# Sparse attention and a feed-forward layer: another PSUM bank for one first product, and two gates kept in SBUF

## The chip, the cores and the metric

The kernel runs on one core of a Trainium2 chip. The metric is the device time of one execution in microseconds (us). The engines go by their names in the profile: PE is TensorE (matmul), PEld its weight load, DVE is VectorE, ACT is ScalarE, POOL is GpSimd, SP is SyncE, from which this kernel issues its DMAs.

## The reference, cut to what matters

Two kinds of sparse attention (heads 0 to 3: a local window of 32 keys; heads 4 to 7: every 32nd key), and behind it a feed-forward layer with a piecewise quadratic gate. The change touches the gate and its neighbours alone.

```python
def _moe_ref(x, w_in, w_out):          # x: 4608 x 512, from the attention
    h = x @ w_in                       # w_in: 512 x 2048
    neg, pos = h <= -1.0, h >= 1.0
    g = np.where(pos, h, np.where(neg, 0.0, (h + 1.0) ** 2 / 4.0))
    return g @ w_out                   # w_out: 2048 x 512
```

## The kernel before

The feed-forward layer works through the 4608 tokens in nine chunks `c` of 512 (`CH`), and in each chunk through the 2048 hidden columns in sixteen blocks `f` of 128 (`NF`). A pair (c, f) is called a unit here; "unit 2" is (0, 2), the third of the first chunk.

A unit has three steps. `up` (line 530) forms the **first product** h in one PSUM bank of 128 x 512: four slices of the contraction, each in three parts (high x high, high x low, low x high, since every float32 is split in two parts of the type fp32r), so 12 matmuls, all of line 540. `gate` (line 543) turns h into the gate: ACT forms u = relu(0.5 h + 0.5) (L549) and squares it (L550), DVE forms g = min(max(h, 1), u) (L554), a copy gives the high part gh (L558 on DVE in chunk 0, L556 on ACT later), and DVE subtracts to get the low part gl (L559). `down` (line 562) forms the **second product**: for each of four groups `t` of 128 tokens, three matmuls into a bank of its own (L570); the four banks gather over all 16 units of a chunk.

PSUM has eight banks, in three pools: four under the name "o", two under "h", two under "a". A pool gives its banks out in turn, and the first write into a bank waits until the last reader of its tenant before is done. Before the change, all first products use the two "h" banks in turn. So unit 2's first product takes the bank of unit 0's, and waits until unit 0's gate has read it. In chunk 0 the four "o" banks serve the attention of the first sequence before the second products begin; their last tenants there are the transposes of `f3` and the values of `v2`.

Where g is written decides who reads the bank last. In unit 0, g is written over u, in SBUF, so L554 is the last reader of h. In every other unit, g is written back over h, in PSUM, and L558 (or L556) and L559 read it there too. The buffer u exists once (`bufs=1`), so ACT's L549 of a unit waits for the last reader of u in the unit before.

Everything is issued in an order written out by hand. In chunk 0, `begin` issues the attention of the first sequence, with the first products of units 0 and 1 mixed in. Then, for each f from 2, PE gets the first product of unit f, the attention steps of `STEPS` (in unit 2: `s0`, the scores of the second sequence), and the second product of the unit two before it (unit 0's, once three gates are pending). DVE gets, for the gate of unit 2, ahead of L554 the steps `m0` and `x0`, which are the mask addition that takes these scores out of PSUM (L353, two instructions) and the maximum (L364). Between the gates ACT, DVE and POOL also turn the weights from the input's 64-bit form into two fp32r parts: L178 and L181 (ACT), L186 (DVE), L191 (POOL), L197 (ACT, or DVE), L201 (DVE), one chain for each half of a block. Each engine takes its instructions strictly in this order, so a matmul that waits holds everything behind it on PE.

Of the kernel before, what the change touches and what calls it, by code (L numbers as in the profile page):

```python
# [17 lines left out]
P = 128  # L18
# [5 lines left out]
def tile_sparse_attention_then_ffn(  # L24
# [29 lines left out]
    B, _, _, _, S = qk_l.shape  # L54
# [5 lines left out]
    CH = 512  # L60
# [46 lines left out]
    def psum(kind, shape, name):  # L107
        pool, bufs = ps[kind]
        return pool.tile(shape, F32, tag=kind, bufs=bufs, name=name)
# [418 lines left out]
    o_ps = {}  # L528

    def up(c, f, first=True, last=True):  # L530
        r0 = c * CH % RING
        if first:
            o_ps[c, f] = psum("h", [P, CH], f"h_{c}_{f}")
        todo = [(cc, x, y) for cc in range(NC) for x, y in HI_LO]
        if not (first and last):

            todo = [(cc, 0, y) for cc in ((0, 1) if first else (2, 3)) for y in range(2)]
            todo += [] if first else [(cc, 1, 0) for cc in range(NC)]
        for n, (cc, x, y) in enumerate(todo):
            nc.tensor.matmul(o_ps[c, f], wt[f][:, x, 0, cc * P:(cc + 1) * P], xT[y][:, cc, r0:r0 + CH],  # L540
                             start=first and n == 0, stop=last and n == len(todo) - 1)

    def gate(c, f, between=lambda: None):

        hp = o_ps.pop((c, f))
        gh = g_p.tile([P, CH], F32R, tag="gh", name=f"gh_{c}_{f}")
        gl = g_p.tile([P, CH], F32R, tag="gl", name=f"gl_{c}_{f}")
        u = g_p.tile([P, CH], F32, tag="u", bufs=1, name=f"u_{c}_{f}")
        nc.scalar.activation(u, hp, AF.Relu, bias=half, scale=0.5)  # L549
        nc.scalar.activation(u, u, AF.Square)  # L550
        between()

        g = u if (c, f) == (0, 0) else hp
        nc.vector.scalar_tensor_tensor(out=g, in0=hp, scalar=1.0, in1=u, op0=ALU.max, op1=ALU.min)  # L554
        if c:
            nc.scalar.copy(gh, g)  # L556
        else:
            nc.vector.tensor_copy(gh, g)  # L558
        nc.vector.tensor_tensor(out=gl, in0=g, in1=gh.bitcast(F32), op=ALU.subtract)  # L559
        return gh, gl  # L560
# [30 lines left out]
    def begin(names):  # L591


        conv = {"A": lambda f, i: conv_a(f, i, (False,)), "L": lambda f, i: conv_a(f, i, (True,)),
                "B": conv_b, "C": conv_c, "D": conv_d, "E": conv_e,
                "G": lambda f, i: conv_d(f, i, nc.vector.tensor_copy)}
        for name in names.split():
            if name[0] in "UV":
                up(0, int(name[0] == "V"), name[1] == "0", name[1] == "1")
            elif name[0] in conv:  # L600
                conv[name[0]](int(name[1]), int(name[2]))
            else:
                first(name)

    with tc.manual_schedule():
# [36 lines left out]
        for c in range(NCH):  # L642
            b = need[c + 1] if c + 1 < NCH and need[c + 1] > need[c] else None
            go = attention(b, lambda u, kind, n: "a") if b is not None else None
            for f in range(NF):
                if c or f > 1:
                    up(c, f)
                pe, pre, mid, post = (LATER if c else STEPS).get(f, ("",) * 4) if b is not None else ("",) * 4
                if pe:
                    go(pe)  # L650
                if c == 0:
                    start_w(*halves[f])
                if pre:
                    go(pre)
                pend.append((c, f, gate(c, f, lambda: mid and go(mid))))
                if c == 0:
                    end_w(*halves[f])
                    if f == 9:
                        for i in range(2):
                            load_piece(NF - 2, i)  # L660
                        for i, k in ((0, 0), (0, 1), (1, 0)):
                            load_piece(NF - 1, i, k, o_p, "ob", 2)
                    if f == NF - 4:
                        load_piece(NF - 1, 1, 1, of=2)
                    if f == NF - 3:
                        fetch_qk(2, 0)
                if post:
                    go(post)
                n = 2 if 0 < c and (c, f) < (NCH - 1, NF - 1) else 1
                if len(pend) > 2:  # L670
                    down(*pend[:n])
                    del pend[:n]
# [61 lines left out]
```

## Time and profile before

| | us |
|---|---|
| time, median of 3 runs (lowest, highest) | 881.38 (881.37, 883.25) |
| the profiled execution, its own time | 883.73 |
| its span in the profile | 881.9 |
| PE busy | 872.9 |
| ACT busy | 398.0 |
| DVE busy | 384.6 |
| POOL busy | 114.7 |

The span is what the profiler saw between the first and the last instruction; the execution's own time includes 1.8 us around it. A row of the timeline gives the start and the duration in us, the engine, the line of the kernel, the operation, output and input by their names, the shapes, and how many instructions the row holds (x4); square brackets give the idle time ahead of it and what ended that. Matmuls overlap each other in the pipeline, so a row of four that takes 1.07 us holds four starts 0.23 us apart and the duration of the last. A row of the windows gives the stretch, its length, the busy time and the count of PE, PEld, DVE, ACT and POOL, then the granted clock of PE (1.00 is full), the busy share of the DMA engines and GB/s. A row of the groups gives the count, and the shortest, median and longest duration in ns.

### The profile page before, as it was taken

What the parts mean: (1) busy time and instruction counts of PE and PEld (TensorE: products, weight loads), DVE (VectorE), ACT (ScalarE), POOL (GpSimd) and SP (SyncE); (2) the same over time, 40 slices, a digit from 0 to 9 for tenths busy, and PEclk for the clock granted to TensorE, in tenths of its full rate; (3) what the DMA queues carried; (4) which work ended last, traced back from release to release, by engine and by line L of the source; (5) the groups of instructions that cost most, each with busy time, mean ns of one, the idle gap of its engine ahead of it and who ended that gap; (6) DMA issues with size and microseconds to landing.
All of it is one profiled execution on the core that took longest, in us unless ns stands there. A gap on an engine that the chain in (4) does not pass through costs nothing.

```text
span 881.9 us, 17353 instructions
## 1 busy us (share of the span) xinstructions
PE 872.9 (99%) x7253; PEld 710.3 (81%) x7253; DVE 384.6 (44%) x709; ACT 398.0 (45%) x732; POOL 114.7 (13%) x136
## 2 busy tenths in 40 slices
PE   8999999999999999999999999999999999999998
PEld 6788888888888888887888888888888888888886
DVE  5899854443453434434344345333453322222221
ACT  5889953434434443334434343444333433343333
POOL 6354411100120002100110011100210000000000
PEclk8999999999999999999999999999999999999999
DMA  9917331422232322421241223321222000000001
GB/s 354 405 65 242 114 121 61 140 59 60 105 100 81 83 70 72 125 64 62 81 145 52 67 105 94 87 82 49 76 82 60 33 29 1 0 35 14 1 0 48
DMA packets 41646, 77.61 MB, mean 88 GB/s; under 512 B 8800, under 2 KB 22112, under 8 KB 41568
## 3 DMA queue, kind: packets, MB, share of 16 engines
q1 hardware_dynamic: 41568, 76.50, 26.8%
q8 instruction: 57, 0.93, 0.4%
q14 instruction: 21, 0.17, 0.1%
HBM read 59.18 MB, written 17.30 MB: 87 GB/s over the span
## 4 chain that ended last, share of the span: by engine, by line
PE 95%; DMA 1%; ACT 1%; DVE 1%; SPq 1%; issue 0%; ACTq 0%; DVEq 0%
PE o L570 44%; PE h L540 44%; PE xp L459 3%; PE sc L302 3%; DMA qk<-in_qk_s 1%; PE tp L405 1%; SPq L443 0%; DMA pT<-there 0%; ACT u L549 0%; ACT u L550 0%; DMA there<-t 0%; DVE xTl L504 0%; DVE h L554 0%; SPq L237 0%; ACT gh L556 0%
## 5 line engine op out<-in xcount | busy, mean ns | idle before, releaser
L540 PE MATMUL h<-xTh,w 128*128 128x512 f32 x1152 | 373.2, 391 | 0.4 <-DVE u L554 0.4
L570 PE MATMUL o<-w,gh 128*128 128x512 f32 x1152 | 359.5, 393 | 0.1
L554 DVE SCALAR_TENSOR_TENSOR h<-h,u 128x512 f32<-128x512 f32 x143 | 100.0, 699 | 377.1 <-ACT u L550 377.0
L540 PEld LDWEIGHTS h<-xTh,w 128*128 128x128 f32 x1152 | 216.3, 188 | 46.6 <-DVE u L554 0.8
L570 PEld LDWEIGHTS o<-w,gh 128*128 128x128 f32 x1152 | 213.4, 188 | 45.3 <-ACT gh L556 0.6
L540 PE MATMUL h<-xTl,w 128*128 128x512 f32 x576 | 224.5, 390 | 0.4 <-DVE xTl L504 0.4
L570 PE MATMUL o<-w,gl 128*128 128x512 f32 x576 | 224.9, 390 | 0.0
L549 ACT ACTIVATE u<-h,half 128x512 f32<-128x512 f32 x144 | 99.1, 688 | 269.6 <-PE h L540 268.6
L559 DVE TENSOR_TENSOR gl<-h,gh 128x512 fp32r<-128x512 f32 x143 | 98.9, 692 | 84.6 <-ACT gh L556 83.7
L570 PEld LDWEIGHTS o<-w,gl 128*128 128x128 f32 x576 | 108.1, 188 | 25.7 <-DVE gl L559 0.6
L540 PEld LDWEIGHTS h<-xTl,w 128*128 128x128 f32 x576 | 108.1, 188 | 22.9 <-DVE xTl L504 1.1
L556 ACT CAST gh<-h 128x512 fp32r<-128x512 f32 x128 | 75.2, 587 | 100.1 <-DVE h L554 100.1
L550 ACT ACTIVATE u<-u 128x512 f32<-128x512 f32 x144 | 91.0, 632 | 4.6
L368 POOL TENSOR_TENSOR pr<-pr,st 128x768 f32<-128x768 f32 (+3 forms) x31 | 36.3, 1172 | 322.8 <-DVE st L364 307.6
L392 POOL TENSOR_TENSOR pr<-pr,st 128x648 f32<-128x648 f32 (+3 forms) x30 | 35.2, 1173 | 119.3 <-DVE st L391 118.4
L191 POOL TENSOR_TENSOR raw<-raw 128x512 uint32<-128x512 uint32 (+1 forms) x34 | 35.0, 1047 | 37.9 <-DVE raw L186 23.4
L504 DVE TENSOR_TENSOR xTl<-xp,xTh 128x216 fp32r<-128x216 f32 (+8 forms) x94 | 35.7, 442 | 6.0 <-ACT xTh L500 6.0
L383 ACT ACTIVATE st<-st 128x12 f32<-128x12 f32 (+2 forms) x32 | 6.8, 211 | 67.5 <-DVE st L379 67.4
L459 PEld LDWEIGHTS xp<-pT,v 64*64 64x64 f32 (+2 forms) x1760 | 29.0, 138 | 10.1 <-issue 8.2
L302 PEld LDWEIGHTS sc<-qk 64*32 64x32 f32 (+1 forms) x1856 | 25.9, 117 | 12.1 <-issue 10.1
L459 PE MATMUL xp<-pT,v 64*64 64x32 f32 (+2 forms) x1760 | 32.3, 224 | 1.5 <-DMA pT<-there 0.8
L500 ACT CAST xTh<-xp 128x216 fp32r<-128x216 f32 (+8 forms) x94 | 31.1, 459 | 6.0 <-DVE xTl L504 3.5
(56 smaller groups left out, 348.3 us busy)
## 6 DMA issues: line engine op xcount, KB each, us to landing
raw<-in_w SPq DMA_DIRECT2D x30, 512.0 KB, 9.6
qk<-in_qk_s SPq DMA_DIRECT2D x16, 604.0 KB, 4.9
qk<-in_qk_l SPq DMA_DIRECT2D x16, 576.0 KB, 4.8
out<-ob SPq DMA_DIRECT2D x35, 256.0 KB, 2.0
v<-in_v_l SPq DMA_DIRECT2D x21, 384.0 KB, 4.0
there<-t SPq DMA_DIRECT2D x96, 48.0 KB, 1.7
pT<-there SPq DMA_DIRECT2D x12, 384.0 KB, 3.0
v<-in_v_s SPq DMA_DIRECT2D x7, 384.0 KB, 4.4
```

The source lines that it names most:

```text
L302: nc.tensor.matmul(sc[j][i * Q:(i + 1) * Q, s, p], qk[:, 0, q0:q0 + Q], qk[:, 1, k0:k0 + W], start=u not in covered, stop=u not in covered)
L368: eng.tensor_tensor(out=pr, in0=pr, in1=st[:, 0].unsqueeze(2).broadcast_to(list(pr.shape)), op=ALU.add)
L392: eng.tensor_tensor(out=pr, in0=pr, in1=st[:, 2].unsqueeze(2).broadcast_to(list(pr.shape)), op=ALU.mult)
L459: nc.tensor.matmul(xp[p][j * D:(j + 1) * D, n], loaded[b, local, b0 + n][keys, j], qs, start=True, stop=True)
L504: nc.vector.tensor_tensor(out=dst[1], in0=src, in1=dst[0].bitcast(F32), op=ALU.subtract)
L540: nc.tensor.matmul(o_ps[c, f], wt[f][:, x, 0, cc * P:(cc + 1) * P], xT[y][:, cc, r0:r0 + CH], start=first and n == 0, stop=last and n == l ...
L549: nc.scalar.activation(u, hp, AF.Relu, bias=half, scale=0.5)
L550: nc.scalar.activation(u, u, AF.Square)
L554: nc.vector.scalar_tensor_tensor(out=g, in0=hp, scalar=1.0, in1=u, op0=ALU.max, op1=ALU.min)
L556: nc.scalar.copy(gh, g)
L559: nc.vector.tensor_tensor(out=gl, in0=g, in1=gh.bitcast(F32), op=ALU.subtract)
L570: nc.tensor.matmul(o_ps[c][t], gs[x][:, t * P:(t + 1) * P], wt[f][:, y, 1, :], start=f == 0 and n == 0, stop=f == NF - 1 and n == 2)
```

## The change

Two lines. Unit 2's first product is taken from the pool "o", so that it no longer takes the "h" bank of unit 0's; and the gates of units 1 and 2 are written over u in SBUF, as unit 0's is, rather than over h in PSUM.

```diff
     def up(c, f, first=True, last=True):
         r0 = c * CH % RING
         if first:
-            o_ps[c, f] = psum("h", [P, CH], f"h_{c}_{f}")
+            o_ps[c, f] = psum("o" if (c, f) == (0, 2) else "h", [P, CH], f"h_{c}_{f}")
...
-        g = u if (c, f) == (0, 0) else hp
+        g = u if (c, f) < (0, 3) else hp
         nc.vector.scalar_tensor_tensor(out=g, in0=hp, scalar=1.0, in1=u, op0=ALU.max, op1=ALU.min)
         if c:
             nc.scalar.copy(gh, g)
         else:
             nc.vector.tensor_copy(gh, g)
         nc.vector.tensor_tensor(out=gl, in0=g, in1=gh.bitcast(F32), op=ALU.subtract)
```

No instruction is added, removed or put elsewhere on any engine; what changes is who waits for whom. In the rows below, h_1, h_2 and h_3 are the first products of units 1, 2 and 3, w the weights, and a name in square brackets is the engine whose semaphore the instruction waits for (DVE_49 is VectorE's).

On PE, at the start of unit 2's first product, behind the last matmuls of unit 1's (- before, + after):

```order
 L540 MATMUL h_1_617<-xTh,w_585 128x512 [waits DVE_49]
 L540 MATMUL h_1_617<-xTh,w_585 128x512 x3
+L540 MATMUL h_2_697<-xTh,w_643 128x512 [waits PE_49,Activation_49]
+L540 MATMUL h_2_697<-xTl,w_643 128x512
 L540 MATMUL h_2_697<-xTh,w_643 128x512 [waits DVE_49]
-L540 MATMUL h_2_697<-xTl,w_643 128x512
-L540 MATMUL h_2_697<-xTh,w_643 128x512 x2
+L540 MATMUL h_2_697<-xTh,w_643 128x512
```

Before, its first matmul waits for DVE (the gate of unit 0, L554). After, the first matmul waits for PE and ACT alone (the bank's tenants in the attention, and the weights' high part), and the third for DVE (the weights' low part, L201).

On PE, in unit 0's second product and the start of unit 3's first (o_0 to o_3 are the four banks of the second products):

```order
-L570 MATMUL o_1_788<-w_524,gh_0_654 128x512 x2
+L570 MATMUL o_1_788<-w_524,gh_0_654 128x512 [waits PE_49]
+L570 MATMUL o_1_788<-w_524,gh_0_654 128x512
 L570 MATMUL o_1_788<-w_524,gl_0_655 128x512
 L570 MATMUL o_2_789<-w_524,gh_0_654 128x512 [waits PE_49]
 L570 MATMUL o_2_789<-w_524,gh_0_654 128x512
 L570 MATMUL o_2_789<-w_524,gl_0_655 128x512
-L570 MATMUL o_3_790<-w_524,gh_0_654 128x512 [waits PE_49]
+L570 MATMUL o_3_790<-w_524,gh_0_654 128x512 [waits DVE_49]
 L570 MATMUL o_3_790<-w_524,gh_0_654 128x512
 L570 MATMUL o_3_790<-w_524,gl_0_655 128x512
```

With unit 2's first product in front of them in the pool, the four second products move on by one bank, and the fourth comes round to the bank of unit 2's first product. Its first matmul now waits for DVE, for the instruction that reads that bank last: L554 of unit 2. Before, it waited for PE's own earlier work in the bank.

On DVE, from the gate of unit 1 to that of unit 2, after the change (gh and gl are the two parts of the gate, raw the weights as they come, pr the scores in SBUF, sc the scores in PSUM, st the maxima):

```order
L554 SCALAR_TENSOR_TENSOR u_1_686<-h_1_617,u_1_686 128x512 [waits DVE_49,Activation_49]
L558 CAST gh_1_684<-u_1_686 128x512 [waits DVE_49]
L559 TENSOR_TENSOR gl_1_685<-u_1_686,gh_1_684 128x512 [waits DVE_49]
L201 TENSOR_TENSOR w_692<-raw_183,w_692 128x512 [waits Activation_49]
L201 TENSOR_TENSOR w_585<-raw_172,w_585 128x512 [waits Activation_49]
L186 TENSOR_SCALAR raw_190<-raw_190 128x512 [waits DMAHW2_49,Activation_49]
L186 TENSOR_SCALAR raw_178<-raw_178 128x512 [waits DMAHW5_49,Activation_49]
L353 TENSOR_TENSOR pr_0_773<-sc_0_0_710,m_loc 128x384 [waits PE_49]
L353 TENSOR_TENSOR pr_0_773<-sc_0_1_711,m_loc 128x384 [waits PE_49]
L364 TENSOR_REDUCE st_0_774<-pr_0_773 128x12 [waits DVE_49]
L554 SCALAR_TENSOR_TENSOR u_2_770<-h_2_697,u_2_770 128x512 [waits Activation_49]
```

The order of these eleven rows is that of before. In the first three and the last, u stands where h stood.

## The prediction

> **What bounds the kernel now.** I read the page first: engines, then the chain that ended last.
>
> ```profile
> PE 872.9 (99%) x7253; PEld 710.3 (81%) x7253; DVE 384.6 (44%) x709; ACT 398.0 (45%) x732; POOL 114.7 (13%) x136
> PE 95%; DMA 1%; ACT 1%; DVE 1%; SPq 1%; issue 0%; ACTq 0%; DVEq 0%
> ```
>
> PE is the bound: 95% of the chain. So the question is in which places PE stands still, and whether a place comes or goes. The windows and the waits of PE answer that for everything behind the change:
>
> ```profile
> 42.00:870.00 828.00, 827.23 (x6538) 675.50 (x6537) 354.22 (x649) 365.18 (x664) 94.08 (x96) 1.00 0.24 73
> ```
>
> ```profile
> PE xp L459 <- DMA pT<-there: 0.8, 1, 0.8
> ```
>
> From 42 us to 870 us PE is busy for 827.23 of 828 us at full clock, and has one wait, of 0.8 us. What PE loses before 42 us is therefore not made good later (at most 0.8 us of it), and what it gains there is kept. The place itself, in order of time on PE:
>
> ```profile
> 31.02 1.07 PE L540 MATMUL h<-xTh,w 128*128 128x512 f32 x4
> 32.44 0.50 PE L540 MATMUL h<-xTh,w 128*128 128x512 f32 x1 [0.35 <-DVE u L554]
> 32.78 0.39 PE L540 MATMUL h<-xTl,w 128*128 128x512 f32 x1
> 33.01 0.62 PE L540 MATMUL h<-xTh,w 128*128 128x512 f32 x2
> ...
> 35.39 1.17 PE L302 MATMUL sc<-qk 64*32 64x64 f32 x96
> 36.49 0.72 PE L570 MATMUL o<-w,gh 128*128 128x512 f32 x2
> ...
> 38.44 0.40 PE L570 MATMUL o<-w,gl 128*128 128x512 f32 x1
> 38.67 0.62 PE L570 MATMUL o<-w,gh 128*128 128x512 f32 x2
> 39.13 0.39 PE L570 MATMUL o<-w,gl 128*128 128x512 f32 x1
> ```
>
> Unit 1's first product ends with the four matmuls from 31.02; unit 2's begins at 32.44, held until the gate of unit 0 (L554) has left its bank. Then come 96 scores (35.39) and unit 0's second product, four banks of three matmuls each; the fourth bank's three begin at 38.67. Next, VectorE over the same stretch:
>
> ```profile
> 31.70 0.69 DVE L554 SCALAR_TENSOR_TENSOR u<-h,u 128x512 f32<-128x512 f32 x1 [1.37 <-ACT u L550]
> ...
> 35.74 0.70 DVE L554 SCALAR_TENSOR_TENSOR h<-h,u 128x512 f32<-128x512 f32 x1 [0.89 <-ACT u L550]
> 36.47 0.69 DVE L558 CAST gh<-h 128x512 fp32r<-128x512 f32 x1
> 37.20 0.69 DVE L559 TENSOR_TENSOR gl<-h,gh 128x512 fp32r<-128x512 f32 x1
> 37.81 1.28 DVE L201 TENSOR_TENSOR w<-raw,w 128x512 fp32r<-128x512 f32 x2
> 39.01 0.76 DVE L186 TENSOR_SCALAR raw<-raw 128x512 uint32<-128x512 uint32 x2
> 39.68 1.01 DVE L353 TENSOR_TENSOR pr<-sc,m_loc 128x384 f32<-128x384 f32 x2
> 40.72 0.95 DVE L364 TENSOR_REDUCE st<-pr 128x12 f32<-128x768 f32 x1
> 41.59 0.69 DVE L554 SCALAR_TENSOR_TENSOR h<-h,u 128x512 f32<-128x512 f32 x1
> ```
>
> The three L554 rows are the gates of units 0, 1 and 2. From 35.74 to 42.28 VectorE has no gap; its only idle times are ahead of the first two gates, which wait for ScalarE. Unit 2's gate is late because nine other instructions stand between it and unit 1's.
>
> **Term 1, the wait that goes.** Four matmuls from 31.02 at the usual spacing of 0.23 us (32.78 to 33.01) end their slots at 31.93. Unit 2's first product, no longer behind unit 0's gate, could start there and not at 32.44: 0.51 us. The first matmul after the wait is followed 0.34 us later rather than 0.23, another 0.11. So 0.6 us of PE time comes free, and scores and unit 0's second product move up by as much: the fourth bank would be due at 38.67 - 0.62 = 38.05, and the third bank's last matmul would end near 38.2.
>
> **Term 2, the wait that comes.** The pool of the second products has four banks, given out in turn. Unit 2's first product takes one, the second products then take the other three and, as fourth, the very bank of unit 2's first product. The rows of the changed program say so: the fourth bank's first matmul now waits for VectorE. The last to read that bank is L554 of unit 2, which in the trace begins at 41.59 and ends at 42.28. From the end of a gate to the matmul it frees took 0.05 us (31.70 + 0.69 = 32.39, then 32.44). So the fourth bank starts near 42.33. Against 38.67 that is 3.66 us late, and with 0.11 us for the first matmul after a wait **3.8 us**. Term 1 is inside this: it makes PE arrive earlier at a wait whose end VectorE sets, and so is worth nothing. PE stands from 38.2 to 42.3, 4.1 us.
>
> Can VectorE come sooner? The gates in SBUF speed up one instruction, the cast:
>
> ```profile
> L558 DVE CAST gh<-h x4: 690/691/692, 36.5 to 54.5; 128x512 fp32r<-128x512 f32 x4
> L558 DVE CAST gh<-u x1: 426/426/426, 32.4 to 32.4; 128x512 fp32r<-128x512 f32 x1
> ```
>
> That is 0.26 us for unit 1 ahead of unit 2's gate (unit 2's own cast comes behind it). But GpSimd runs when unit 1's cast starts, and another VectorE instruction that met it was held:
>
> ```profile
> 34.64 2.10 POOL L191 TENSOR_TENSOR raw<-raw 128x512 uint32<-128x512 uint32 x2 [3.14 <-DVE raw L186]
> ```
>
> ```profile
> 51.62 1.48 POOL L392 TENSOR_TENSOR pr<-pr,st 128x768 f32<-128x768 f32 x1 [2.69 <-DVE st L391]
> ```
>
> ```profile
> L186 DVE TENSOR_SCALAR raw<-raw x1: 1705/1705/1705, 51.7 to 51.7; 128x512 uint32<-128x512 uint32 x1
> ```
>
> The L186 at 51.7 took 1.705 us, to 0.3 us behind the end of L392 at 53.10; the pair at 39.01 took 0.76 in all. L191 runs to 36.74; a cast held from 36.47 to there and then 0.43 long ends at 37.17, against 37.16 before. So the gain is between 0 and 0.26, and I take 0, since the cast's start lies inside L191. Term 2 is 3.5 to 3.8. L554 and L559 cost the same from either memory (0.69, 0.70 in the rows above). The buffer u is now read until L559, which a later gate's ScalarE pass must await; unit 1's L559 ends at 37.89, and unit 2's pass at L549 stands behind ScalarE's own work until 39.59 (L550 follows and ends at 40.95, before 41.59). No cost while ScalarE is that late; if it were free at once, the wait would end at 37.89 and still be hidden.
>
> Behind the waiting matmul stand the rest of the fourth bank, unit 3's first product, 48 scores and every later product; who waits for them:
>
> ```profile
> 41.85 0.39 PE L540 MATMUL h<-xTh,w 128*128 128x512 f32 x1
> 42.17 0.77 PE L302 MATMUL sc<-qk 64*32 64x64 f32 x48
> ```
>
> ```profile
> 45.27 0.68 ACT L549 ACTIVATE u<-h,half 128x512 f32<-128x512 f32 x1
> ```
>
> Unit 3's last matmul moves from 41.85 to about 45.6 and ends near 46.0, so ScalarE's pass of unit 3 moves from 45.27 by 0.7; the mask addition for the scores, VectorE's, by a few tenths. Both slip far less than PE does, so they are earlier relative to PE than before, and no further wait follows from them. No DMA changes place.
>
> **Term 3, the clock.** PE stands still for longer than anywhere in the trace. What a thin stretch did before:
>
> ```profile
> 6.31:9.73 3.42, 2.50 (x146) 2.03 (x146) 2.44 (x4) 0.90 (x5) 1.22 (x4) 1.00 1.02 394
> ...
> 13.14:16.56 3.42, 2.02 (x37) 1.40 (x39) 3.39 (x7) 3.36 (x10) 1.26 (x2) 1.00 1.02 393
> 16.56:19.97 3.41, 3.11 (x89) 2.64 (x82) 1.89 (x7) 2.82 (x8) 1.35 (x2) 0.50 1.03 417
> 19.97:23.39 3.42, 3.42 (x57) 3.36 (x58) 3.03 (x9) 1.28 (x4) 2.14 (x2) 0.50 1.03 409
> 23.39:26.80 3.41, 3.41 (x99) 2.80 (x98) 2.21 (x7) 2.64 (x8) 1.15 (x1) 1.00 1.03 415
> ```
>
> The granted clock halves at 16.56, behind a stretch with PE busy for 2.02 of 3.42 us, and is back at 23.39, 6.83 us later, twice 3.41; a stretch with 2.50 busy had left it alone. A standstill of 4.1 us leaves at least one stretch of 3.41 us with 1.4 us of work or less, wherever its borders fall. I therefore take the clock to halve. The price of half clock, from transposes at either rate:
>
> ```profile
> 21.46 2.34 PE L405 MATMUL tp<-ident,pr 128*128 128x128 f32 x11
> ...
> 53.91 0.82 PE L405 MATMUL tp<-ident,pr 128*128 128x128 f32 x6
> ```
>
> One takes 0.213 us in the first row (clock 0.50 but for its end) and 0.137 in the second (clock 1.00), so 36% of the work is lost at least, and half where matmuls follow each other closely, as here. One stretch of 3.41 us at half clock costs 1.2 to 1.7 us of PE time. The bounds are 0 (no drop) and 2.7 (low from 42.3 for 5.5 us, when the stretch that holds the restart is too thin to bring the clock back). I take 1.6, one full stretch near half.
>
> **Sum.** 3.8 + 1.6 = 5.4 us. Against the profiled execution's 883.73 us (span 881.9) that is 889.1; that execution lies 2.4 us above the median of the runs shown, so against 881.38 us the forecast is **886.8 us**.
>
> **Rivals.**
> *The clock stays up*: 3.8 us alone, 885.2 us (884.9 with the cast's full gain). For it speaks the end of the span:
>
> ```profile
> 876.73:880.14 3.41, 1.48 (x7) 0.89 (x5) 0.00 (x0) 1.86 (x5) 0.00 (x0) 1.00 0.75 274
> 880.14:881.90 1.76, 0.00 (x0) 0.00 (x0) 0.00 (x0) 0.00 (x0) 0.00 (x0) 1.00 0.21 65
> ```
>
> A stretch with 1.48 us of work was not followed by a lower clock in the record. Against it: 2.02 us of work was followed by one at 16.56, though of smaller matmuls. [...]
>
> *The new wait finds its gate done*: then only term 1 is left, 0.6 us faster, 880.8 us. Its place is the fourth bank, due at 38.05; it decides if unit 2's gate ends by 38.0. That needs VectorE 4.3 us earlier than the trace, with nine instructions of 5.1 us between it and the gate before (36.44 to 41.59); it could only be if waits, not work, filled that time, and their rows show no gap.
>
> *VectorE meets GpSimd more often*:
>
> ```profile
> 39.56 2.10 POOL L191 TENSOR_TENSOR raw<-raw 128x512 uint32<-128x512 uint32 x2 [2.82 <-ACT raw L178]
> ```
>
> The second of the L186 pair, if some tenths of a microsecond move either engine, could fall behind the first of these L191 and be held by its 1.05 us. Then the standstill ends near 43.4: 4.8 + 1.6, 887.8 us.
>
> **How the numbers follow.** The forecast has 0.52, the clock that stays up 0.36, the longer VectorE chain 0.06, the gate found done 0.04, anything else 0.02. The range runs from 884.5 (3.5 us, no drop, less some tenths between runs) to 887.9 (3.8 + 2.7). A change of 0.3%, 2.6 us, is about what a measurement of this kernel can tell from none. All cases but the gate found done lie above 884.0: slower 0.90; same 0.06 (a standstill shorter by over 1 us); faster 0.04.
>
> **What would show it.** In the new profile PE waits once, about 4 us, at L570 for DVE u L554 with its end near 42.3; the wait of L540 at 32.4 is gone; unit 2's first product starts near 31.9; the granted clock shows 0.5 for 3 to 5 us behind it. Without the dip, term 3 is wrong. If the wait ends before 41 us, the VectorE order was read wrongly; if PE idles less than before between 42 and 870 us, the loss is paid back.

## The result, and the profile after

The changed kernel takes 887.29 us (median of 4 runs, 886.25 to 889.18), the kernel before 882.32 us beside it (4 runs, 881.37 to 883.44). The ratio is 1.0065, with a 95% interval of 1.0052 to 1.0078: slower by 4.6 to 6.9 us. The forecast was 886.8 us, in a range of 884.5 to 887.9. The profiled execution took 887.41 us, with a span of 885.6.

The page of the changed kernel, engines and the costliest group of second products (busy time, mean ns, then the idle time ahead of it and what ended most of that):

```profile
PE 872.0 (98%) x7253; PEld 709.4 (80%) x7253; DVE 383.7 (43%) x709; ACT 397.7 (45%) x732; POOL 114.5 (13%) x136
...
L570 PE MATMUL o<-w,gh 128*128 128x512 f32 x1152 | 360.1, 394 | 4.1 <-DVE u L554 4.0
```

PE is as busy as before (872.0 against 872.9 us) in a span 3.7 us longer, and the second products, which had 0.1 us of idle time ahead of them, now have 4.1. The waits of PE say that this is one wait:

```profile
PE o L570 <- DVE u L554: 4.0, 1, 4.0
```

PE in order of time in the changed kernel, from the end of unit 1's first product to the scores behind unit 3's:

```profile
30.36 0.61 PE L540 MATMUL h<-xTh,w 128*128 128x512 f32 x2
30.82 0.39 PE L540 MATMUL h<-xTl,w 128*128 128x512 f32 x1
...
32.72 1.17 PE L302 MATMUL sc<-qk 64*32 64x64 f32 x96
33.82 0.72 PE L570 MATMUL o<-w,gh 128*128 128x512 f32 x2
...
35.77 0.40 PE L570 MATMUL o<-w,gl 128*128 128x512 f32 x1
40.17 1.22 PE L570 MATMUL o<-w,gh 128*128 128x512 f32 x2 [4.00 <-DVE u L554]
41.19 0.63 PE L570 MATMUL o<-w,gl 128*128 128x512 f32 x1
41.62 0.63 PE L540 MATMUL h<-xTh,w 128*128 128x512 f32 x1
42.04 0.63 PE L540 MATMUL h<-xTl,w 128*128 128x512 f32 x1
...
46.27 0.77 PE L302 MATMUL sc<-qk 64*32 64x64 f32 x48
```

No gap stands ahead of unit 2's first product any more. Three banks of unit 0's second product pass, and the fourth begins at 40.17 after 4.00 us. Behind it the matmuls start 0.42 us apart (41.62 to 42.04) where 0.23 is usual, so PE runs at about half its rate. VectorE over the same time:

```profile
33.70 0.69 DVE L554 SCALAR_TENSOR_TENSOR u<-h,u 128x512 f32<-128x512 f32 x1 [0.88 <-ACT u L550]
34.43 0.57 DVE L558 CAST gh<-u 128x512 fp32r<-128x512 f32 x1
...
38.57 0.95 DVE L364 TENSOR_REDUCE st<-pr 128x12 f32<-128x768 f32 x1
39.44 0.68 DVE L554 SCALAR_TENSOR_TENSOR u<-h,u 128x512 f32<-128x512 f32 x1
40.15 1.27 DVE L558 CAST gh<-u 128x512 fp32r<-128x512 f32 x1
```

Unit 2's gate ends at 40.12, 0.05 us before the fourth bank starts. From unit 1's gate to unit 2's are 5.74 us, 5.85 before. The granted clock (the number before the last two) in stretches of the changed kernel:

```profile
37.00:38.00 1.00, 0.00 (x0) 0.00 (x0) 1.00 (x4) 1.00 (x3) 0.60 (x1) 1.00 0.98 385
38.00:39.00 1.00, 0.00 (x0) 0.00 (x0) 0.96 (x3) 0.97 (x3) 1.00 (x2) 0.83 1.05 422
39.00:40.00 1.00, 0.00 (x0) 0.00 (x0) 1.00 (x2) 0.92 (x2) 0.83 (x2) 0.50 1.04 406
...
42.00:45.00 3.00, 3.00 (x8) 2.31 (x7) 2.89 (x6) 1.20 (x2) 1.17 (x2) 0.50 0.78 311
45.00:46.00 1.00, 1.00 (x5) 0.73 (x3) 0.00 (x0) 0.00 (x0) 0.92 (x1) 0.75 0.09 37
```

It halves at 38.66, in the middle of the wait (0.83 in that stretch: 0.66 us at 1.00, 0.34 at 0.50), and is back at 45.5. That is 6.8 us, two times the 3.41 us that a fall lasts in e8 (below). PE works at half clock in the last 5.3 us of it, from 40.17 to 45.5.

One thing makes the two spans hard to compare. In the profiled execution of the kernel before, the clock was also down from 16.56 to 23.39; in that of the changed kernel it was not (1.00 up to 38 us), so everything near 32 us comes about 2 us earlier in it. To leave this out I measure within each profile, from the scores of unit 2's step to those of four steps later (L302, 48 of 64x54). Before, these stand at 35.39 (shown in the prediction) and here:

```profile
60.12 0.92 PE L302 MATMUL sc<-qk 64*64 64x54 f32 x48
```

In the changed kernel the first set stands at 32.72 (above) and the second here:

```profile
64.20 0.92 PE L302 MATMUL sc<-qk 64*64 64x54 f32 x48
```

That is 24.73 us before and 31.48 after, 6.75 more. Unit 2's scores come 0.6 us sooner than they did (0.98 us ahead of unit 1's gate, 0.35 before), so the change costs 6.1 us over this stretch. Behind it, the two kernels run in step: the lag of the changed one stays at 4.07 to 4.09 us of the trace's time from 60 to 396 us, and at 3.83 to 3.84 from 412 us on. (It is less than 6.1 because the profile of the kernel before had lost some 2 us to its early low clock.)

### The profile page after: what moved, and what is told of

Same layout as the page of the kernel before. It is cut to its first block, busy times and chain, and to the rows that moved or that the text cites. A ratio compares the mean times of both kernels' runs of the same rounds, so it can differ in the third digit from the quotient of the medians.

```text
span 885.6 us, 17353 instructions
## 1 busy us (share of the span) xinstructions
PE 872.0 (98%) x7253; PEld 709.4 (80%) x7253; DVE 383.7 (43%) x709; ACT 397.7 (45%) x732; POOL 114.5 (13%) x136
## 4 chain that ended last, share of the span: by engine, by line
PE 94%; DMA 2%; DVE 1%; ACT 1%; SPq 1%; issue 0%; ACTq 0%; DVEq 0%
PE o L570 44%; PE h L540 44%; PE xp L459 3%; PE sc L302 3%; DMA qk<-in_qk_s 1%; PE tp L405 0%; SPq L443 0%; DMA pT<-there 0%; DMA v<-in_v_s 0%; ACT u L549 0%; ACT u L550 0%; DVE pr L353 0%; ACT raw L181 0%; DVE st L364 0%; DMA there<-t 0%
## 5 line engine op out<-in xcount | busy, mean ns | idle before, releaser
L554 DVE SCALAR_TENSOR_TENSOR h<-h,u 128x512 f32<-128x512 f32 x141 | 98.6, 699 | 379.3 <-ACT u L550 379.2
L559 DVE TENSOR_TENSOR gl<-h,gh 128x512 fp32r<-128x512 f32 x141 | 97.6, 692 | 84.9 <-ACT gh L556 83.7
L459 PEld LDWEIGHTS xp<-pT,v 64*64 64x64 f32 (+2 forms) x1760 | 28.2, 134 | 10.4 <-issue 8.6
L302 PEld LDWEIGHTS sc<-qk 64*32 64x32 f32 (+1 forms) x1856 | 25.7, 116 | 12.3 <-issue 9.4
L459 PE MATMUL xp<-pT,v 64*64 64x32 f32 (+2 forms) x1760 | 31.6, 221 | 1.8 <-ACT pT L415 0.7
```

The costliest lines, as they stand in the source:

```text
L302: nc.tensor.matmul(sc[j][i * Q:(i + 1) * Q, s, p], qk[:, 0, q0:q0 + Q], qk[:, 1, k0:k0 + W], start=u not in covered, stop=u not in covered)
L459: nc.tensor.matmul(xp[p][j * D:(j + 1) * D, n], loaded[b, local, b0 + n][keys, j], qs, start=True, stop=True)
```

## The experiments

The last column of this table is the same measure for every profile: the time between the two sets of scores, less 24.73, and less the 0.62 of term 1 where unit 2's first product uses the other bank (there the first set comes that much sooner, which lengthens the time between the sets and is no loss).

| kernel | median us (runs) | ratio to before, 95% interval | between the scores, us | cost there, us |
|---|---|---|---|---|
| before | 881.5 to 882.3 in three sets | | 24.73 | |
| changed | 887.29 (4) | 1.0052 to 1.0078 | 31.48 | +6.1 |
| e1, bank alone | 889.8 (6) | 1.0064 to 1.0105 | 32.42 | +7.1 |
| e2, gates alone | 881.76 (12) | 0.9986 to 1.0009 | 24.77 | 0.0 |
| e3, wait filled | 886.48 (8) | 1.0028 to 1.0058 | 29.08 | +3.7 |
| e4, gate first | 886.68 (6) | 1.0046 to 1.0083 | 29.29 | +3.9 |
| e5, bank later | 882.63 (12) | 0.9990 to 1.0015 | 25.24 | -0.1 |
| e6, before, early places filled | 882.16 (11) | 0.9994 to 1.0012 | 24.77 | 0.0 |
| e8, changed, early places filled | 887.39 (5) | 1.0052 to 1.0077 | 30.64 | +5.3 |
| e9, both fillings | 886.71 (5) | 1.0042 to 1.0069 | 29.05 | +3.7 |

The theory: the loss is PE's wait at the fourth bank for unit 2's gate, and a halved clock behind that wait. The first rival: the gates in SBUF cost it. The second: the wait is all, and the clock is a symptom.

### e1: the bank alone

```diff
-        g = u if (c, f) < (0, 3) else hp
+        g = u if (c, f) == (0, 0) else hp
```

> The bank alone: unit 2's first product in the fourth bank of the second products, the gates of units 1 and 2 written over h in PSUM as before. Theory (the loss is PE's wait for the last reader of that bank, and a halved clock behind it): the last reader is now L559 of unit 2, two instructions of 0.69 us behind L554, so PE stands about 1.4 us longer than the 4.0 us of the changed kernel, and the time is 888.7 us (887.8 to 889.8) against 887.3. Rival (the loss comes from gates in SBUF that meet GpSimd): without those gates the time falls back to 882.3 to 884.

889.8 us, at the upper end of the range expected, and in the waits of e1 on PE:

```profile
PE o L570 <- DVE gl L559: 5.6, 1, 5.6
```

With g in PSUM, the bank is free only after L559 and the wait is 1.6 us longer, in the place that the theory names. The gates in SBUF do not cause the loss; they shorten it (6.1 us over the stretch with them, 7.1 without).

### e2: the gates alone

```diff
-            o_ps[c, f] = psum("o" if (c, f) == (0, 2) else "h", [P, CH], f"h_{c}_{f}")
+            o_ps[c, f] = psum("h", [P, CH], f"h_{c}_{f}")
```

> The gates of units 1 and 2 in SBUF alone, unit 2's first product in the bank of unit 0's as before. Theory (the bank is what costs): no wait at the fourth bank, the 0.35 us wait for unit 0's gate stays, and the time is that of before, 882.3 us (881.4 to 883.2). Rival (gates in SBUF cost): 884 us or more.

881.76 us, no difference from before, no wait at the fourth bank, and the old one of 0.3 us for unit 0's gate:

```profile
PE h L540 <- DVE u L554: 0.3, 1, 0.3
```

Together with e1 this puts the whole loss on the bank.

### e3: the wait filled with matmuls

```diff
-        if first:
+        if first and (c, f) not in o_ps:
...
+            if (c, f0, t) == (0, 0, 3):
+                o_ps[0, 3] = psum("h", [P, CH], "h_0_3")
+                for _ in range(32):
+                    nc.tensor.matmul(o_ps[0, 3][:, :256], zeros, zeros[:, :1].broadcast_to([P, 256]), start=True, stop=True)
```

> The changed kernel with 32 matmuls of zeros, 128 x 256, set ahead of the fourth bank's first matmul, into the bank that unit 3's first product takes next: PE waits for the same gate, but is busy meanwhile. Theory (two prices, the wait of 3.5 us and the halved clock of 2.5 us): the fourth bank starts as late as before, the granted clock stays at 1.00, and the time is 884.8 us (883.8 to 885.8). Rival (the wait alone is the loss, and the clock costs nothing beside it): 887.3 us as the changed kernel (886.5 or more).

PE in e3, around the fourth bank:

```profile
38.18 3.73 PE L571 MATMUL h<-zeros 128*128 128x256 bf16 x32
42.32 0.74 PE L574 MATMUL o<-w,gh 128*128 128x512 f32 x2 [0.41 <-DVE u L554]
42.90 0.40 PE L574 MATMUL o<-w,gl 128*128 128x512 f32 x1
43.14 0.40 PE L540 MATMUL h<-xTh,w 128*128 128x512 f32 x1
43.37 0.40 PE L540 MATMUL h<-xTl,w 128*128 128x512 f32 x1
```

The bank still waits for the gate, but the matmuls behind it start 0.23 us apart: the clock stays up, at 1.00 from 36 to 50 us. The cost over the stretch falls from 6.1 to 3.7 us, as the theory said. So the wait itself is worth 3.7 us and the clock, in the changed kernel's profile, 2.4. The median, 886.48, lies above the 883.8 to 885.8 that I expected and 0.02 us short of the rival's 886.5, so it does not decide between them. The expectation left out the early fall of the clock. The eight runs fall in two groups: four with a mean clock of 0.999 or 1.000 take 884.4 to 885.8 us, four with 0.996 take 887.1 to 887.7 (see e6); the profile shown is of the second group.

### e4: the gate of unit 2 first

```diff
-        STEPS = {2: ("s0", "", "m0 x0", "a0"), 3: ("s1", "e0 q0", "p0 m1 x1", "a1 r0"), 4: ("", "e1 q1", "p1", "r1"),
+        STEPS = {2: ("s0", "", "", "m0 x0 a0"), 3: ("s1", "e0 q0", "p0 m1 x1", "a1 r0"), 4: ("", "e1 q1", "p1", "r1"),
...
+                if (c, f) == (0, 2):
+                    pend.append((c, f, gate(c, f)))
                 if c == 0:
                     start_w(*halves[f])
...
-                pend.append((c, f, gate(c, f, lambda: mid and go(mid))))
+                if (c, f) != (0, 2):
+                    pend.append((c, f, gate(c, f, lambda: mid and go(mid))))
```

> The changed kernel with the gate of unit 2 issued ahead of the weight conversions of that step on ScalarE, VectorE and GpSimd, and the mask addition and maximum (L353, L364) behind the gate. Theory (the place of unit 2's gate in VectorE's order sets how long PE stands): ScalarE's passes of unit 2 come some 2.2 us sooner, L554 of unit 2 ends about 2.7 us sooner, PE stands 1.2 to 1.6 us instead of 4.0, the clock stays at 1.00 behind it, and the time is 883.5 us (882.3 to 884.8), if the conversions put off by 2 us are not late for PE. Rival (the standstill has another end than that gate): 4.0 us as before and 887.3.

The wait is shorter, as it should be if the place of the gate sets it; the waits and the clock of e4:

```profile
PE o L570 <- DVE u L554: 1.8, 1, 1.8
```

```profile
39.00:40.00 1.00, 1.00 (x5) 0.80 (x4) 1.00 (x3) 0.78 (x2) 0.07 (x1) 0.76 1.04 414
40.00:42.00 2.00, 2.00 (x6) 1.52 (x5) 0.36 (x2) 0.68 (x1) 2.00 (x2) 0.50 1.02 406
42.00:43.00 1.00, 1.00 (x4) 0.79 (x3) 0.81 (x2) 0.95 (x2) 0.01 (x1) 0.53 1.02 406
```

But the clock fell all the same, at 39.5 and for 3.4 us, and PE then waited 0.5 us in two places for the mask addition that had been put off. 3.9 us in the stretch and 886.68 us instead of 883.5: a miss. The part on the wait held (1.8 us for 4.0, with 1.2 to 1.6 expected), the part on the clock did not. Nor is the clock the whole of the miss: one of the six runs has a mean clock of 1.000 and still took 885.44 us. What else cost time there stays open.

### e5: the fourth bank later

```diff
+    late = []
...
+            if (c, f0, t) == (0, 0, 3):
+                late.append(units[0])
+                continue
-            for _, f, gs in units:
+            for _, f, gs in [*(late.pop() for _ in range(len(late) if t == 3 else 0)), *units]:
...
+                if (c, f) == (0, 3):
+                    down(pend.pop(0))
```

> The changed kernel with the three matmuls of unit 0 in the fourth bank put off until unit 1's second product reaches that bank, behind unit 3's first product and its scores (the second product of unit 1 stands at the same place of PE's order). Theory (PE only waits because the fourth bank comes up too soon): PE has 5.6 us of other matmuls first, the gate of unit 2 is done when the bank comes up, no standstill, the clock stays up, and the 0.6 us that unit 2's first product starts earlier is kept: 881.7 us (880.9 to 882.6). Rival (PE meets the next wait instead, for weights or for a gate): 883.5 us or more, with that wait in the trace.

No wait at the fourth bank, and the clock does not fall there (1.00 from 24 to 50 us): the loss of 6 us is gone, which shows that the bank came up too soon. But the time is that of before, not 0.6 us less. In e5, PE's weight loads at the start of unit 5's first product:

```profile
50.86 0.19 PEld L541 LDWEIGHTS h<-xTh,w 128*128 128x128 f32 x1 [0.50 <-ACT raw L178]
51.39 0.30 PEld L541 LDWEIGHTS h<-xTh,w 128*128 128x128 f32 x2 [0.24 <-DVE w L201]
```

Unit 2's second product still starts 0.6 us earlier than before (47.90 against 48.46). Here PE waits for the weights that ACT and DVE convert: 0.3 us of the head start is left at the first row (50.89 on PE against 51.18), 0.1 us behind unit 5's first product (53.78 against 53.91), and at 67 us PE is 0.1 us late (66.72 against 66.63). The rival was right in kind, PE met the next wait; its 883.5 us did not come, and 882.63 lies just above the range of the theory. A head start of 0.6 us on PE is worth nothing here, where DVE is busy for 96% and ACT for 78% of the time from 45 to 61 us.

### e6, e8, e9: the early fall of the clock kept out

The edit below, made to the kernel before (e6), to the changed kernel (e8) and to e3 (e9):

```diff
-            Zf0:9 w0 g3 p1 x3 e2 Zf0:5 L00 f0 B00 b3 C00 c0 e3 v0 q2 w1 f1 p2 r2 L10 A10 q3 d1 v1 f2
+            Zf0:9 w0 g3 p1 x3 e2 Zf0:11 L00 f0 B00 b3 C00 c0 e3 Zv0:6 v0 q2 w1 f1 p2 r2 L10 A10 q3 d1 v1 f2
```

> The kernel before the change, with 12 more matmuls of zeros, six in each of two idle places of PE in the attention of the first sequence (0.64 us near 13.7 and 0.68 us near 15.1). Theory (executions of one kernel differ by 2 us because those idle places let the clock halve near 16.6 in some executions and not in others): the granted clock stays at 1.00 up to 24 us, all executions lie near 881.0 us (880.7 to 882.2), none near 883.5, and the median is 881.1. Rival (the two times have another cause): the executions still fall in two groups, at 881 and 883.5.

> The changed kernel with the same 12 matmuls of zeros in the two early idle places. If they keep the early clock up, the only fall left is that behind the wait at the fourth bank. Theory (wait 3.6 us, clock 2.4 us): 887.1 us (886.4 to 887.8), 6.0 above the kernel before with the same filling. Rival (the clock falls behind the wait in some executions only, as it does early on): two groups, near 884.7 and 887.2.

> The changed kernel with both fillings, the 12 matmuls of zeros in the early idle places and the 32 in the wait at the fourth bank. Theory (the wait's own price, without any fall of the clock): 884.9 us (884.4 to 885.6), 3.7 above the kernel before with the early filling, and 2.3 below the changed kernel with it. Rival (zeros in the wait cost more than they save): 886 us or more.

In e6's profile the clock stays at 1.00 up to 24 us:

```profile
0.00:24.00 24.00, 21.32 (x546) 16.73 (x546) 15.38 (x34) 14.13 (x36) 15.14 (x35) 1.00 0.93 357
```

Of its 11 runs none is above 882.57 us. Of the runs of the kernel before, 11 of 25 (beside e1, e2, e3 and e5) and 2 of 16 (beside e4, e6, e8 and e9) lie at 883.1 to 885.4, all with a mean clock of 0.994 to 0.998. The 16 runs beside e6 hold too few of these to settle it alone. With the profiles it is well supported: that of the kernel before shows the early fall and took 883.73 us, that of e2 does not and took 882.03. Not all of it is explained: 5 of the 11 runs lie above the 882.2 expected, and one of them has a mean clock of 0.997. e6 is no better version either: its median is 882.16 against 881.49, and the gain expected in it did not come; in its profile PE waits 1.5 us for the transposed probabilities (L459) where before waited 0.8.

e8 takes 887.39 us, in the range expected, 5.2 us above e6; none of its runs is near the 884.7 of the rival. The changed kernel's own profile was already without the early fall, so e8's profile is a second execution with the same wait of 4.00 us. It costs 5.3 us in the stretch, with a low clock of 3.4 us rather than 6.8:

```profile
40.00:41.00 1.00, 1.00 (x4) 0.82 (x5) 1.00 (x1) 1.00 (x3) 0.93 (x1) 0.79 1.05 418
41.00:43.00 2.00, 2.00 (x6) 1.58 (x5) 1.97 (x4) 1.97 (x4) 0.00 (x0) 0.50 1.01 401
43.00:44.00 1.00, 1.00 (x4) 0.78 (x3) 1.00 (x4) 0.00 (x0) 0.39 (x1) 0.50 0.93 373
44.00:46.00 2.00, 2.00 (x55) 1.42 (x54) 0.70 (x2) 0.69 (x1) 1.71 (x2) 1.00 0.29 119
```

e9 repeats e3's 3.7 us. Its median of 886.71 misses the 884.9 expected and lies where the rival put it (886 or more), only 0.7 us below e8. The filling does save 1.6 us in the stretch (5.3 to 3.7), but in e9's profile waits for the transposed probabilities between 200 and 510 us, far behind the change, take as much back (0.3 us in e8):

```profile
PE xp L459 <- DMA pT<-there: 2.0, 3, 0.9
```

Why these come and go between 0.2 us (e3) and 2.0 us (e9) stays open, and so does whether the fillings have a part in it.

## Where the prediction was right, and which step failed

**The likeliest case came**: the wait and the halved clock, 5.4 us forecast, 5.3 (e8) to 6.1 us (changed kernel) within the profiles, 5.0 us between the medians. That the forecast of 886.8 us came within 0.5 us of the measured 887.29 is in part luck: in the changed kernel's profile the sum lacks 0.7 us of 6.1, because term 3 is 0.8 us too small, and the median that it was added to is itself 0.9 us below the one measured beside the changed kernel.

**Term 2, the wait that comes**, was right in place, cause and size. PE stood 4.00 us (4.1 forecast), its end came 0.05 us behind L554 of unit 2, and the price with the clock up is 3.7 us in e3 and e9 against 3.8 forecast. The wait did end before 41 us, at 40.17, which the prediction named as the sign that VectorE's order was read wrongly. It was not: without the early low clock all of this came 2 us sooner, and unit 2's gate began 5.74 us behind unit 1's, 5.85 before. The cast of unit 1 was held by GpSimd in part: 0.57 us, between the 0.43 alone and the 0.69 before, so 0.1 us of the 0.26 was gained where I took none. The prediction let a held cast take 0.43 us behind GpSimd's end; it ended 0.28 us behind it (35.00 against 34.72).

**Term 1, the wait that goes**, was right in that it vanished within term 2. But the sentence ahead of it, that what PE gains before 42 us is kept, was wrong: e5 has the gain without the loss, and by 67 us nothing of it is left, most of it lost to the conversion of the weights. A trace in which PE never waits does not show that PE could go sooner; another engine may be just in time. The forecast did not rest on it, but the rival of 880.8 us did, and e5, at 882.63, speaks against that time.

**Term 3, the clock**, is the step that failed: right in kind and mis-sized. It took one full stretch of 3.41 us at half clock, 1.6 us, as the likely case. In the changed kernel's own profile the clock stayed down for two stretches, 5.3 us of them with PE at work, worth 2.4 us (6.1 less e3's 3.7); the sign named was 3 to 5 us. The prediction had this as its upper bound, 2.7 us, but gave no reason to take the single stretch. How the one case differs from the other shows when the wait is laid out in stretches of 3.41 us, first the changed kernel, then e8:

```profile
35.25:38.66 3.41, 0.92 (x4) 0.40 (x3) 3.38 (x8) 3.38 (x7) 1.26 (x2) 1.00 1.02 399
38.66:42.07 3.41, 1.90 (x5) 1.51 (x6) 3.34 (x5) 3.33 (x7) 2.31 (x2) 0.50 1.03 407
```

```profile
37.17:40.58 3.41, 0.62 (x3) 0.53 (x4) 3.34 (x6) 3.32 (x7) 3.21 (x3) 1.00 1.04 410
40.58:43.99 3.41, 3.41 (x10) 2.67 (x9) 3.38 (x7) 2.39 (x4) 0.72 (x2) 0.50 0.99 395
43.99:47.41 3.42, 3.42 (x61) 2.58 (x60) 2.07 (x6) 2.08 (x5) 1.72 (x2) 1.00 0.38 111
```

In the changed kernel the clock fell inside the wait. PE restarted at 40.17 and was busy for only 1.90 us of that stretch, and the clock stayed down for the whole next one. In e8 PE restarted at 39.96 and the clock fell 0.6 us behind that; the stretch at half clock was full of work, and the clock came back after it, for 1.6 us (5.3 less 3.7), the size forecast. In e1's profile, with PE busy for 0.49 us in the first stretch, two stretches came as well. The mean clock of e8's five runs speaks for both cases in one kernel: three at 0.998, as in the profile, take 886.2 to 887.4 us, two at 0.995 and 0.996 take 888.3 and 888.4. So the same wait of 4.00 us cost one stretch in e8, where the fall came behind PE's restart, and two in the changed kernel, where it came ahead of it. In these three profiles and in e4's, the clock came back behind a stretch with PE busy throughout (3.41 of 3.41 us in e8 and e4, 3.42 of 3.42 in the changed kernel and e1). Whether the place of the fall decides was not tested by itself.

The rival in which the clock stays up (885.2 us) did not come in any profile with the wait in it; with the clock held up by zeros (e3 without the early fall, 884.4 to 885.8 us) its time was about right.

**The basis** was the other weak place. I set the sum on the median of three runs, 881.38, and noted that the profiled execution lay 2.4 us higher without asking why. The reason stood in the rows of term 3: that execution had the early fall. Runs of the same kernel beside the experiments with a mean clock of 0.999 or more take 880.8 to 882.9 us, those with 0.995 take 883.1 to 883.9, and the median of a few runs depends on how many of each it holds: 882.3, 882.3 and 881.5 in the three sets here.

## What to carry to other kernels

When a tile moves to another bank of a rotating pool, look for the next tenant of that bank, and at what stands ahead of the last reader on its engine; the wait that the move removes may be worth less than the one it creates, as here. A standstill of PE may have to be priced twice, once as time and once as the clock behind it (here it fell behind 1.8 us of standstill in e4 as behind 4.0), and the second price differed between executions of one kernel (mean clock 0.998 or 0.995 in e8); matmuls of zeros set into the wait told the two apart (e3: 3.7 and 2.4 us). And before a gain on the busiest engine is counted, ask which other engine is only just in time for it (in e5, 0.6 us gained on PE was gone 20 us later).

## What the runs showed of the hardware

In e4 the clock fell behind a standstill of 1.8 us, with 1.64 us of work in the 3.41 us ahead of the fall:

```profile
36.11:39.52 3.41, 1.64 (x7) 1.01 (x7) 3.07 (x6) 3.30 (x6) 0.00 (x0) 1.00 1.03 403
```

Before the change it fell at 16.56 with no wait of PE longer than 1.0 us ahead of it; the 3.41 us up to the fall held 2.01 us of work, in smaller matmuls. A stretch with 2.21 us of work (e8, 33.75 to 37.17) left the clock at 1.00. In every profile with a fall ahead of the last products it stayed down for one stretch of 3.41 us (e4, e8) or for two (before, changed, e1, e3, e5).

Two VectorE casts from SBUF to SBUF that started while GpSimd was at work took longer in the changed kernel's profile than unit 0's, which started at 30.39 with GpSimd idle and took 0.43 us. GpSimd at the casts of units 1 and 2:

```profile
32.62 2.10 POOL L191 TENSOR_TENSOR raw<-raw 128x512 uint32<-128x512 uint32 x2 [3.19 <-DMA raw<-in_w]
```

```profile
39.66 1.48 POOL L368 TENSOR_TENSOR pr<-pr,st 128x768 f32<-128x768 f32 x1 [0.17 <-DVE st L364]
```

Unit 1's cast (34.43) took 0.57 us and unit 2's (40.15, both shown above) 1.27, each to 0.28 us behind GpSimd's end. It cost nothing here, because PE takes up unit 2's gate only at 52.54 us.
